# Output projection of a gated layer: weights stationary, 512 tokens of gated values moving, result written feature by token

## The chip, the core and the metric

The kernel runs on one core of one Trainium2 chip. The core has TensorE (PE) for matrix products into PSUM, with its weight loads shown apart (PEld), VectorE (DVE), ScalarE (ACT), GpSimd (POOL) and SyncE (SP), and 16 DMA engines that move data between HBM and SBUF. DMA transfers are issued here by SP and POOL. The metric is the device time of one execution in microseconds (us), median of several runs. The profile is of one further execution.

## The reference

Attention in chunks of 64 tokens, then two feed-forward layers on 4608 tokens of 512 features:

```python
attn = softmax(scale * q_c @ k_c.T); x = attn @ v_c        # chunks of 64
h = x @ w_in;  g = where(h > 0, h, exp(min(h, 0)) - 1)     # 512 -> 2048
x = g @ w_out                                              # 2048 -> 512
gate = 1 / (1 + exp(-(x @ w_gate)));  val = x @ w_val      # 512 -> 1536 each
out = (gate * val) @ w_out2                                # 1536 -> 512
```

The result is a float32 array of 4608 tokens by 512 features.

## The kernel before

Every product of the layers is computed with seven block products instead of eight (a Strassen scheme): both operands are cut in two halves each way, sums of the blocks are formed, and the seven results are added into four output blocks. The factors are float32, each split into a high part of type float32r and the rest; a product makes three passes (high x high, low weight x high, high weight x low), `PASSES` (line 34).

The weights are converted from float64 early on, summed for the seven products (`sums`, `sums_of_sums`, lines 249 to 272), split and written to DRAM (`wd`). `hold` (line 326) reads them back through POOL's queue ahead of their use, in tiles of 512 KB, up to `room` of them; all other tiles of at most 1024 float32 a partition (`four`) come out of the same 28 buffers (`w_p`), so `room(...)` is 28 less what those take. Larger tiles come out of ten slots of 2048 float32 (`get` and `free`, lines 362 to 370), which are handed round in turn; a tile in a slot waits until everything that used the slot before is done, a store from it too.

Tokens are worked in five blocks, four of 2 x 512 tokens and a last one of 2 x 256 (`NLS`, line 48).

- Stage 1, attention and the first layer, and stage 2, the second layer (`stage_2`, line 693). Its `product` (line 724) has the weights as the stationary operand and 512 tokens moving (256 in the short block). `split_b` makes the high part with a cast on ACT and the low part with a subtraction on DVE (`split`, line 99; the lines 95 and 101 in the profile), one product ahead of its use; `sub_b` makes the sums of blocks on DVE, `after` takes a finished product out of PSUM, and `beside` says what is issued after each part of a product. Everything is issued in the order in which the code calls it; each engine works in that order.
- Stage 3, the gated layer (`unit`, line 860): 30 units of seven products each; from unit 18 on units of 512 and of 256 tokens alternate. Unit 27 has 512 tokens, units 28 and 29 have 256. A unit ends with `finish` (line 944), which multiplies and stores the gated values to DRAM (`gvd`); it is run in the unit after, behind that unit's second product, on POOL for unit 28 and on DVE for 27 and 29. After each product `hold` is called with the room that the tiles of the moment leave.
- Stage 4, the output projection (`stages_3_4`, line 954). The block is cut into nine groups of 256 tokens (twice, for the two halves). Here the *gated values* are the stationary operand, 128 tokens at a time, and the weights move, 256 columns at a time (line 1022): 6 x 3 x 2 = 36 matmuls a product. A product fills one of the two banks of its PSUM tile, and groups take turns. `prepare` (line 983) makes the next product's split and sums just before a product is issued; a split is two tiles, one of 1024 and one of 512 elements a partition. The result is token by feature and is stored in rows of 2 KB. The first group's loads, sums and first split are placed into the last units of stage 3 (line 1064).

PSUM holds four tiles (`bank_x`, `w`, `y`, `z`) of two banks each; the seven products use x, w, y, z, x, y, z. A bank can be written again only when what it held has been read.

Of the kernel before, what the change touches and what calls it, by code (L numbers as in the profile page):

```python
# [18 lines left out]
DM = H * D  # L19
# [37 lines left out]
RIGHT = (0, 4, 3, 5, 1, 2, 6)  # L57
# [3 lines left out]
def kernel(  # L61
# [18 lines left out]
        for m, n in (("mid", QM), ("glu", QU), ("out2", QU // 2))  # L80
# [115 lines left out]
    def convert_pairs(which, queue_of):  # L196
# [52 lines left out]
        def sums(p):  # L249
            now[p, "s"] = alloc("s", F32)  # L250
            t, s = quarters(p, "t"), quarters(p, "s")
            if tiles_of[p][3]:
                nc.vector.tensor_add(out=s[:, 0], in0=t[:, 3], in1=t[:, 2])
                nc.vector.tensor_sub(out=s[:, 2], in0=t[:, 0], in1=t[:, 3])
            elif p < HF:
                nc.vector.tensor_add(out=s[:, 0], in0=t[:, 0], in1=t[:, 3])
                nc.vector.tensor_sub(out=s[:, 2], in0=t[:, 1], in1=t[:, 0])
            else:
                nc.vector.tensor_sub(out=s[:, 0], in0=t[:, 0], in1=t[:, 1])
                nc.vector.tensor_sub(out=s[:, 2], in0=t[:, 3], in1=t[:, 0])  # L260

        def sums_of_sums(p):
# [4 lines left out]
            elif p < HF:  # L267
                nc.vector.tensor_sub(out=s[:, 1], in0=s[:, 0], in1=t[:, 1])
                nc.vector.tensor_sub(out=s[:, 3], in0=t[:, 2], in1=s[:, 1])
            else:  # L270
                nc.vector.tensor_sub(out=s[:, 1], in0=t[:, 3], in1=s[:, 0])
# [51 lines left out]
    uses += 2 * [("out2", r, i) for i in range(7) for r in range(QU // 2)]  # L323
    held = {}

    def hold(at, room, ahead):
# [8 lines left out]
        for k in need:  # L335
            if not made(k):
                break
            if k not in held:
# [4 lines left out]
                nc.gpsimd.dma_start(out=t, in_=wd[m][q][:, (RIGHT if m == "out2" else LEFT)[i]])  # L343
# [349 lines left out]
    def stage_2(one):  # L693

        raw, gc, three = {}, {}, {}
        KEYS = {"b11": (0, 0), "b21": (1, 0), "b12": (0, 1), "b22": (1, 1)}
        FROM = ("b11", "t2", "b11", "b12", "b21", "b22", "b21")

        def load_b(j, k):
            if j is None:  # L700
                return
            par, h = KEYS[k]
            blk, c = divmod(START[j] + h * NLS[j], TB)
            for s in range(2):
                t = raw[j, k, s] = get(k, (HF // 2, NLS[j]))
                nc.sync.dma_start(out=t, in_=gd[blk][:, par, 4 * s:4 * s + 4, c:c + NLS[j]])

        def sub_b(j, out, a, b, s):
            if j is None:
                return  # L710
            if (j, out, s) not in raw:
                raw[j, out, s] = get(out, (HF // 2, NLS[j]))
            nc.vector.tensor_sub(out=raw[j, out, s], in0=raw[j, a, s], in1=raw[j, b, s])

        def split_b(j, i, p):
            if j is None:
                return
            for k in range(2):
                t = gc[j, i, 2 * p + k] = four(2, NLS[j], dtype=F32R)
                split(raw[j, FROM[i], p // 2][:, 2 * (p % 2) + k], t[:, 0], t[:, 1], nc.scalar, nc.vector)  # L720
            if i in (2, 3, 5, 6) and p % 2 == 1:
                free(raw.pop((j, FROM[i], p // 2)))

        def product(j, i, p):
            w = held["mid", p, i]
            for k in range(2):
                t = gc.pop((j, i, 2 * p + k))
                for u in range(2):
                    for n, (zw, zx) in enumerate(PASSES):
# [3 lines left out]
                            rhs=t[:, zx],  # L733
                            start=(i < 4 and p == 0 and k == 0 and n == 0),
                            stop=(p == QM - 1 and k == 1 and n == 2),
                            skip_group_check=True,
                        )

        def after(j, i):
            ps = bank[PRODUCTS[i]][:, :, 0:NLS[j]]  # L740

            def new(k):
                three[k] = shaped(three_p.tile([128, 1024], F32, tag="three", name=k), (2, NLS[j]))
                return three[k]

            def store(k, h, e):
                nc.sync.dma_start(out=ymid[j][:, h, e], in_=three.pop(k))
# [20 lines left out]
        def beside(j, nxt, i, p):  # L768

            h, odd = p // 2, p % 2 == 1  # L770
            if i == 0:
                if not odd:
                    sub_b(j, "t2", "b22", "b11", h)
                split_b(j, 1, p)
                if j == 0 and p == 3:
                    load_b(0, "b21")
            elif i == 1:
                split_b(j, 2, p)
                if odd:
                    sub_b(j, "b12", "b22", "b12", h)  # L780
            elif i == 2:
                if p == 0:
                    load_b(nxt, "b11")
                split_b(j, 3, p)
            elif i == 3:
                if p == 0:
                    load_b(nxt, "b12")
                split_b(j, 4, p)
            elif i == 4:
                if not odd:  # L790
                    sub_b(j, "b21", "b21", "t2", h)
                    free(raw.pop((j, "t2", h)))
                split_b(j, 5, p)
                if p == 3:
                    load_b(nxt, "b22")
            elif i == 5:
                if p == 0:
                    load_b(nxt, "b21")
                split_b(j, 6, p)
            else:  # L800
                split_b(nxt, 0, p)
                if odd:
                    sub_b(nxt, "b11", "b12", "b11", h)
# [18 lines left out]
        for n in range(HF):  # L822
            one(end - HF + n, True)
            if n in (0, 2, 4):
                load_b(0, ("b11", "b12", "b22")[n // 2])
            if 2 <= n <= 5:
                split_b(0, 0, n - 2)
            if n >= 6:
                sub_b(0, "b11", "b12", "b11", n - 6)
            hold(0, room(F1 - 2 * n - 2, 8), SLACK + 1 + n)  # L830
        for o, j in enumerate(ORDER):
            nxt = ORDER[o + 1] if o + 1 < NJ else None
            for i in range(7):
                for p in range(QM):
                    product(j, i, p)
                    if o == i == p == 0:
# [3 lines left out]
                        three_p = ctx.enter_context(  # L840
                            tc.tile_pool(name="three", bufs=3, side="right", reuse_waits="tile")
                        )
                    beside(j, nxt, i, p)
# [10 lines left out]
                after(j, i)  # L854
        assert not todo and not raw and not gc
# [296 lines left out]
```

## Time and profile before

| | us |
|---|---|
| median of three runs | 1652.19 (1652.01 to 1654.71) |
| profiled execution, in all | 1653.24 |
| its span in the trace | 1651.5 |
| TensorE busy | 1620.2 |
| VectorE busy | 1204.8 |
| ScalarE busy | 749.6 |
| GpSimd busy | 299.1 |

The span runs from the first to the last instruction that the trace shows; the profiled execution took 1.74 us more than that. The page of the profile lists busy time by engine, the span in 40 slices, the DMA queues, the chain of waits that ended last, and the costliest groups of instructions. The trace behind it can be asked for single stretches, lines, engines and transfers. Matmuls are pipelined, so that one matmul's duration is longer than the distance from its start to the next one's start.

### The profile page before, as it was taken

Reading aid. Unit: us, or ns where it says so; the run is one execution under the profiler, and the core shown is the slowest. Engines: PE = TensorE matmul, PEld = TensorE weight load, DVE = VectorE, ACT = ScalarE, POOL = GpSimd, SP = SyncE. Lnnn points to the kernel's source line nnn. Section 1 sums busy time; section 2 is a strip of 40 time slices with the busy share of each in tenths; the row PEclk is TensorE's granted clock in tenths of the full one; section 3 lists DMA queues with packets and bytes.
Section 4 is the critical chain, followed back from the end, with each engine's and each line's share of the span. In section 5 each row is a group of like instructions: output and inputs, shape, how many; then the busy total and the mean of one; then the engine's idle time right before and its main releaser. Section 6 shows DMA issues by size and latency. Waiting matters only on the chain.

```text
span 1651.5 us, 27371 instructions
## 1 busy us (share of the span) xinstructions
PE 1620.2 (98%) x10644; PEld 1385.6 (84%) x10644; DVE 1204.8 (73%) x1699; ACT 749.6 (45%) x1273; POOL 299.1 (18%) x488
## 2 busy tenths in 40 slices
PE   6899999999999999999999999999999999999998
PEld 4677777777788898888888888888888899999998
DVE  6878888888637689988855676776664457677676
ACT  5766767767644454463532242332321113333332
POOL 3332111122101022222121222222301030000000
PEclk9899999999999999999999999999999999999999
DMA  6568888898887689999699769779746497443531
GB/s 227 198 214 289 295 297 286 276 291 296 280 297 247 215 317 392 378 338 393 215 313 321 250 202 399 259 270 335 242 144 232 149 357 249 155 139 122 167 121 52
DMA packets 176417, 421.76 MB, mean 255 GB/s; under 512 B 13984, under 2 KB 54944, under 8 KB 171168
## 3 DMA queue, kind: packets, MB, share of 16 engines
q0 software_dynamic: 71328, 216.56, 39.4%
q1 hardware_dynamic: 104960, 203.45, 35.8%
q8 instruction: 84, 1.38, 0.3%
q14 instruction: 45, 0.37, 0.1%
HBM read 287.31 MB, written 132.64 MB: 254 GB/s over the span
## 4 chain that ended last, share of the span: by engine, by line
PE 74%; DVE 14%; ACT 8%; issue 2%; DMA 1%; POOL 0%; SPq 0%; ACTq 0%; DVEq 0%; POOLq 0%
PE bank_x L871 9%; PE bank_z L871 9%; PE bank_y L871 9%; PE bank_x L730 6%; PE bank_z L730 6%; PE bank_y L730 6%; PE bank_z L1022 5%; PE bank_x L1022 4%; PE bank_w L871 4%; PE bank_w L730 3%; PE bank_y L1022 3%; PE bank_y L401 3%; DVE elu L424 2%; PE bank_w L1022 2%; PE bank_z L401 2%
## 5 line engine op out<-in xcount | busy, mean ns | idle before, releaser
L95 ACT CAST four<-b 128x512 fp32r<-128x512 f32 (+1 forms) x240 | 128.0, 577 | 79.1 <-PE bank_y L730 20.8
L101 DVE TENSOR_TENSOR four<-b,four 128x512 fp32r<-128x512 f32 (+1 forms) x240 | 140.1, 634 | 30.2 <-ACT four L95 30.1
L871 PE MATMUL bank_z<-four,w 128*128 128x512 f32 (+1 forms) x720 | 157.6, 368 | 0.0
L893 ACT ACTIVATE s<-s 128x512 f32<-128x512 f32 (+1 forms) x60 | 35.4, 590 | 251.3 <-DVE s L104 251.3
L871 PEld LDWEIGHTS bank_z<-four,w 128*128 128x128 f32 x720 | 126.3, 189 | 22.5
L401 PE MATMUL bank_y<-xs,w 128*128 128x512 f32 x576 | 140.5, 399 | 1.4 <-POOL w L167 0.9
L401 PE MATMUL bank_w<-xs,w 128*128 128x512 f32 x576 | 140.7, 399 | 0.0
L401 PE MATMUL bank_z<-xs,w 128*128 128x512 f32 x576 | 139.6, 398 | 0.0
L343 POOL DMA_DIRECT2D w<-wd_glu x156 | 84.6, 546 | 300.7 <-PE bank_x L871 140.5
L401 PEld LDWEIGHTS bank_y<-xs,w 128*128 128x128 f32 x576 | 107.8, 191 | 23.7 <-POOL w L167 1.2
L401 PEld LDWEIGHTS bank_z<-xs,w 128*128 128x128 f32 x576 | 108.0, 191 | 22.0
L401 PEld LDWEIGHTS bank_w<-xs,w 128*128 128x128 f32 x576 | 107.4, 190 | 21.9
L343 POOL DMA_DIRECT2D w<-wd_mid x105 | 56.0, 537 | 265.9 <-PE bank_x L730 93.7
L730 PE MATMUL bank_x<-four,w 128*128 128x512 f32 (+1 forms) x480 | 100.2, 368 | 0.0
L730 PE MATMUL bank_y<-four,w 128*128 128x512 f32 (+1 forms) x480 | 100.2, 368 | 0.0
L730 PE MATMUL bank_z<-four,w 128*128 128x512 f32 (+1 forms) x480 | 100.2, 368 | 0.0
L730 PEld LDWEIGHTS bank_x<-four,w 128*128 128x128 f32 x480 | 83.7, 189 | 15.0
L730 PEld LDWEIGHTS bank_y<-four,w 128*128 128x128 f32 x480 | 83.7, 189 | 15.0
L730 PEld LDWEIGHTS bank_z<-four,w 128*128 128x128 f32 x480 | 83.7, 189 | 15.0
L104 DVE TENSOR_TENSOR s<-bank_z,s 128x1024 f32<-128x1024 f32 (+1 forms) x60 | 67.0, 1116 | 37.0 <-PE bank_z L871 35.7
L871 PE MATMUL bank_y<-four,w 128*128 128x512 f32 (+1 forms) x432 | 88.5, 354 | 0.0
L871 PE MATMUL bank_x<-four,w 128*128 128x512 f32 (+1 forms) x432 | 88.4, 354 | 0.0
(167 smaller groups left out, 3249.6 us busy)
## 6 DMA issues: line engine op xcount, KB each, us to landing
w<-wd_glu POOLq DMA_DIRECT2D x156, 512.0 KB, 8.2
w<-wd_mid POOLq DMA_DIRECT2D x105, 512.0 KB, 8.3
gd<-elu SPq DMA_DIRECT2D x72, 512.0 KB, 3.6
b<-gd SPq DMA_DIRECT2D x32, 1024.0 KB, 9.2
c<-gv SPq DMA_DIRECT2D x36, 768.0 KB, 5.4
wd_glu<-ch POOLq DMA_DIRECT2D x36, 512.0 KB, 4.8
raw<-in_qkv SPq DMA_DIRECT2D x61, 256.0 KB, 4.0
wd_mid<-ch POOLq DMA_DIRECT2D x24, 512.0 KB, 5.0
```

The costliest lines, as they stand in the source:

```text
L95: nc.scalar.copy(out=out, in_=raw)
L101: lo_eng.tensor_sub(out=lo, in0=raw, in1=hi)
L104: nc.vector.tensor_tensor(out=out, in0=a, in1=b, op=ALU.add)
L343: nc.gpsimd.dma_start(out=t, in_=wd[m][q][:, (RIGHT if m == "out2" else LEFT)[i]])
L401: nc.tensor.matmul(out=h_bank(d)[:, n], lhsT=w[:, zw, kk * 128:(kk + 1) * 128], rhs=xs[j, kk][:, zx], start=(kk == 0 and p == 0), stop=(kk ...
L424: nc.vector.scalar_tensor_tensor(out=e, in0=h_bank(d), scalar=0.0, in1=e, op0=ALU.max, op1=ALU.subtract,)
L730: nc.tensor.matmul(out=bank[PRODUCTS[i]][:, u, 0:NLS[j]], lhsT=w[:, k, zw, 128 * u:128 * u + 128], rhs=t[:, zx], start=(i < 4 and p == 0 a ...
L871: nc.tensor.matmul(out=ps[:, b], lhsT=w[:, b, zw, 128 * k:128 * k + 128], rhs=x_part(j, i, zx, k), start=(i < 4 and k == 0 and p == 0), st ...
L893: nc.scalar.activation(out=x, in_=x if of is None else of, func=ACTF.Sigmoid)
L1022: nc.tensor.matmul(out=po[c][:, m], lhsT=t[:, zx, q % 4, 128 * m:128 * m + 128], rhs=w[:, q % 2, zw], start=(i < 4 and q == 0 and p == 0 a ...
```

## The change

The second layer's routine becomes a class, `Seven`, with the layer's name, its number of weight tiles, and functions that say where a block is read and where a result is written. Stage 2 uses it with four parts, as before; stage 4 now uses it too, with three. In stage 4 the weights are thereby the stationary operand and 512 tokens of gated values move, and the result is feature by token: the kernel's output has the shape 512 by 4608 and is turned on the host when it is returned. The sums of `w_out2` follow the second layer's form (the third branch of `sums` and `sums_of_sums` goes), as many operations as before. A split in stage 4 is one tile of 2 x 512 in a slot, which is freed when its product has been issued. A block of gated values is loaded as a piece of four rows of tiles in a slot and a piece of two in a buffer of `w_p`. Three of those pieces are taken before the units end, so the room for weights in the last units shrinks by one to three. In the last units now stand three splits and a subtraction in two pieces.

```diff
+QO = F2 // 4
-        for m, n in (("mid", QM), ("glu", QU), ("out2", QU // 2))
+        for m, n in (("mid", QM), ("glu", QU), ("out2", QO))
...
-                nc.gpsimd.dma_start(out=t, in_=wd[m][q][:, (RIGHT if m == "out2" else LEFT)[i]])
+                nc.gpsimd.dma_start(out=t, in_=wd[m][q][:, LEFT[i]])
...
+    class Seven:
...
+        def tile(self, j, k, s):
+            n = 2 * min(2, self.parts - 2 * s)
+            return get(k, (n, NLS[j])) if n == 4 else four(n, NLS[j])
...
+        def split(self, j, i, p):
...
+            x = self.raw[j, FROM[i], p // 2][:, 2 * (p % 2):2 * (p % 2) + 2]
+            if self.parts == QM:
+                t = [four(2, NLS[j], dtype=F32R) for k in range(2)]
+                for k in range(2):
+                    split(x[:, k], t[k][:, 0], t[k][:, 1], nc.scalar, nc.vector)
+                self.gc[j, i, p] = t, None
+            else:
+                t = get("gc", (2, 2, NLS[j]), F32R)
+                split(x, t[:, :, 0], t[:, :, 1], nc.scalar, nc.vector)
+                self.gc[j, i, p] = [t[:, 0], t[:, 1]], t
...
+        def product(self, j, i, p):
+            w = held[self.m, p, i]
+            t, slot = self.gc.pop((j, i, p))
             for k in range(2):
                 for u in range(2):
                     for n, (zw, zx) in enumerate(PASSES):
                         nc.tensor.matmul(
                             out=bank[PRODUCTS[i]][:, u, 0:NLS[j]],
                             lhsT=w[:, k, zw, 128 * u:128 * u + 128],
-                            rhs=t[:, zx],
+                            rhs=t[k][:, zx],
...
+            if slot is not None:
+                free(slot)
...
-                parts = 8 + min(7, max(0, 7 * (n - JOINT) + i - 2))
+                parts = 8 + min(8, max(0, 7 * (n - JOINT) + i - 2))
                 if n >= END_WIDE:
-                    parts = 15 - 2 * max(0, i + 1 - XC) if n == END_WIDE else 8 if n == END_WIDE + 1 else 8 - i
+                    parts = (18 - 2 * max(0, i + 1 - XC), 11, 11 - i)[n - END_WIDE]
                 hold(MID + 7 * n + i + 1, room(parts), NW)
...
+        C = {"b21": 0, "b22": 1, "b12": 2, "b11": 3}
+
+        def keep(j, h, e):
+            c = START[j] + h * NLS[j]
+            return out[256 * e:256 * e + 256, c:c + NLS[j]].rearrange("(u p) n -> p u n", p=128)
+
+        z = Seven("out2", QO, lambda j, k, q: gvd[j][:, C[k], q], keep)
         N = len(seq)
         beside = {
-            (N - 4, 0): lambda: load_g(0, "c12"),
-            (N - 3, 0): lambda: load_g(0, "c22"),
-            (N - 3, 4): lambda: load_g(0, "c11"),
-            (N - 2, 0): lambda: load_g(0, "c21"),
-            (N - 2, 3): lambda: sum_1(0),
-            (N - 1, 1): lambda: sum_2(0),
-            (N - 1, 4): lambda: split_g(0, 0, "c11", keep=True),
+            (N - 4, 0): lambda: z.load(0, "b11"),
+            (N - 3, 0): lambda: z.load(0, "b12"),
+            (N - 3, 4): lambda: z.load(0, "b22"),
+            (N - 2, 3): lambda: z.split(0, 0, 0),
+            (N - 2, 5): lambda: z.split(0, 0, 1),
+            (N - 1, 1): lambda: z.split(0, 0, 2),
+            (N - 1, 3): lambda: z.sub(0, "b11", "b12", "b11", 0),
+            (N - 1, 5): lambda: z.sub(0, "b11", "b12", "b11", 1),
         }
...
-        for g in range(G):
+        for j in range(NJ):
+            nxt = j + 1 if j + 1 < NJ else None
             for i in range(7):
-                prepare(g, i)
-                product(g, i)
-                after(g, i)
-                if g == 0:
-                    hold(MID + 7 * N + 3 * (i + 1), room(7), NW)
-                while pending:
-                    pending.pop(0)()
+                for p in range(QO):
+                    z.product(j, i, p)
+                    while pending:
+                        pending.pop(0)()
+                    z.beside(j, nxt, i, p, j == 0)
+                    if j == 0:
+                        hold(MID + 7 * N + 3 * i + p + 1, room(7), NW)
+                z.after(j, i)
...
-    args.append(nc.dram_tensor("out_0", (NT, DM), F32, kind="ExternalOutput").ap())
+    args.append(nc.dram_tensor("out_0", (DM, NT), F32, kind="ExternalOutput").ap())
...
-    return r.results[0]["out_0"]
+    return np.ascontiguousarray(np.asarray(r.results[0]["out_0"]).T)
```

`load`, `sub`, `beside` and `after` of the class are the old functions of stage 2 with the number of parts as a variable.

## Rows read from the trace of the kernel before

**Rows 1.** The page's busy time, share and instructions of each engine.

```profile
PE 1620.2 (98%) x10644; PEld 1385.6 (84%) x10644; DVE 1204.8 (73%) x1699; ACT 749.6 (45%) x1273; POOL 299.1 (18%) x488
```

**Rows 2.** Windows of stages 2 and 4: stretch, length, each engine's busy us.

```profile
core 0: us, PE busy (x) PEld busy (x) DVE busy (x) ACT busy (x) POOL busy (x), PEclk, DMA share, GB/s
505.60:852.00 346.40, 346.40 (x1688) 293.76 (x1687) 292.57 (x394) 172.84 (x319) 70.53 (x130) 1.00 0.90 312
...
1371.00:1647.20 276.20, 275.13 (x2268) 272.70 (x2268) 199.77 (x209) 105.39 (x145) 0.00 (x0) 1.00 0.41 136
```

**Rows 3.** Chain of waits, stages 3 and 4: start, us, what, matmuls.

```profile
1273.72 2.72 PE bank_w L871 x12
...
1351.19 1.44 PE bank_y L871 x12
...
1380.96 4.32 PE bank_y L1022 x36
```

**Rows 4.** The same chain at the passage from stage 3 to 4.

```profile
1362.54 4.41 DMA gv<-s
...
1369.87 1.05 ACT gc L95
```

**Rows 5.** DMA issues at 1353.2, 1353.8 and 1362.5: count, KB, us to landing.

```profile
gv<-s SPq DMA_DIRECT2D x1, 512.0 KB, 8.6
gv<-t SPq DMA_DIRECT2D x1, 512.0 KB, 11.8
...
gv<-s SPq DMA_DIRECT2D x1, 256.0 KB, 7.3
```

**Rows 6.** Groups by line and shape in stage 4: busy, mean ns, idle before.

```profile
L1022 PEld LDWEIGHTS bank_z<-w,gc 128*128 128x128 f32 x432 | 53.6, 191 | 2.2 <-DVE gc L101 2.2
...
L101 DVE TENSOR_TENSOR gc<-c,gc 128x1024 fp32r<-128x1024 f32 x36 | 44.0, 1221 | 36.1 <-ACT gc L95 36.1
L95 ACT CAST gc<-c 128x1024 fp32r<-128x1024 f32 x35 | 36.7, 1049 | 42.6 <-DVE c L992 42.6
...
L101 DVE TENSOR_TENSOR four<-c,four 128x512 fp32r<-128x512 f32 x36 | 24.7, 686 | 0.0
```

**Rows 7.** Groups by line and shape in stage 2.

```profile
L713 DVE TENSOR_TENSOR b<-b,b 128x2048 f32<-128x2048 f32 x15 | 34.3, 2288 | 0.2
...
L104 DVE TENSOR_TENSOR c<-bank_y,u 128x1024 f32<-128x1024 f32 x8 | 9.8, 1220 | 1.1 <-PE bank_y L730 1.1
...
L713 DVE TENSOR_TENSOR b<-b,b 128x1024 f32<-128x1024 f32 x4 | 4.9, 1222 | 0.1
```

**Rows 8.** Timeline of the last two units: start, us, engine, line, operation.

```profile
1354.43 0.69 DVE L104 TENSOR_TENSOR s<-bank_z,s 128x512 f32<-128x512 f32 x1
1355.04 1.75 DVE L977 TENSOR_TENSOR s<-c,c 128x1536 f32<-128x1536 f32 x1
...
1361.97 2.85 DVE L981 TENSOR_TENSOR s<-s,c 128x1536 f32<-128x1536 f32 x1
...
1366.26 0.42 ACT L893 ACTIVATE s<-s 128x256 f32<-128x256 f32 x1 [5.76 <-DVE s L104]
...
1366.98 0.42 DVE L907 TENSOR_TENSOR t<-bank_x,t 128x256 f32<-128x256 f32 x1 [0.76 <-ACT t L893]
1367.02 1.60 PE L871 MATMUL bank_z<-four,w 128*128 128x256 f32 x12
...
1370.82 0.61 ACT L95 CAST four<-c 128x512 fp32r<-128x512 f32 x1
...
1370.96 0.73 PE L1022 MATMUL bank_x<-w,gc 128*128 128x256 f32 x4 [2.35 <-ACT gc L95]
```

**Rows 9.** The end: timeline of the last eviction, and the stores' issues by line.

```profile
1647.15 0.69 DVE L104 TENSOR_TENSOR four<-bank_z,four 128x512 f32<-128x512 f32 x1 [3.62 <-PE bank_z L1022]
...
L1043 SPq DMA_DIRECT2D out<-four x36: 332/351/1256, 1400.0 to 1648.3; - x36
```

**Rows 10.** Windows in the last units, with the DMA share ahead of GB/s.

```profile
1348.00:1358.00 10.00, 10.00 (x85) 9.96 (x84) 7.54 (x9) 2.13 (x5) 4.17 (x8) 1.00 1.13 409
1363.00:1368.00 5.00, 5.00 (x43) 4.90 (x42) 3.54 (x4) 0.69 (x2) 1.92 (x5) 1.00 1.12 402
```

More of the change, by code (lines that the diff above doesn't have):

```diff
@@ L56 @@
 LEFT = (0, 4, 3, 5, 1, 6, 2)
-RIGHT = (0, 4, 3, 5, 1, 2, 6)
 @with_exitstack
@@ L691, in done_x, with __init__, pieces, load @@
             free(xt.pop((j, n)))
[L693 to L699, printed above, removed]
+    KEYS = {"b11": (0, 0), "b21": (1, 0), "b12": (0, 1), "b22": (1, 1)}
+    FROM = ("b11", "t2", "b11", "b12", "b21", "b22", "b21")
+    class Seven:
+        def __init__(self, m, parts, fetch, keep):
+            self.m, self.parts, self.fetch, self.keep = m, parts, fetch, keep
+            self.raw, self.gc, self.three = {}, {}, {}
+        def tile(self, j, k, s):
+            n = 2 * min(2, self.parts - 2 * s)
+            return get(k, (n, NLS[j])) if n == 4 else four(n, NLS[j])
+        def pieces(self):
+            return range((self.parts + 1) // 2)
+        def load(self, j, k):
@@ L700, in load_b @@
             if j is None:
                 return
[L702 to L708, printed above, removed]
+            for s in self.pieces():
+                t = self.raw[j, k, s] = self.tile(j, k, s)
+                nc.sync.dma_start(out=t, in_=self.fetch(j, k, slice(4 * s, 4 * s + t.shape[1])))
@@ L716, in split_b, with ends @@
+        def ends(self, p):
+            return p % 2 == 1 or p == self.parts - 1
+        def split(self, j, i, p):
             if j is None:
                 return
-            for k in range(2):
[L719 to L727, printed above, removed]
+            x = self.raw[j, FROM[i], p // 2][:, 2 * (p % 2):2 * (p % 2) + 2]
[4 more added lines that the diff above has]
+                self.gc[j, i, p] = t, None
+            else:
+                t = get("gc", (2, 2, NLS[j]), F32R)
+                split(x, t[:, :, 0], t[:, :, 1], nc.scalar, nc.vector)
+                self.gc[j, i, p] = [t[:, 0], t[:, 1]], t
+            if i in (2, 3, 5, 6) and self.ends(p):
+                self.release(j, FROM[i], p // 2)
@@ L766, in after, with beside @@
                 store("u", 0, 1)
-        def beside(j, nxt, i, p):
-            h, odd = p // 2, p % 2 == 1
+        def beside(self, j, nxt, i, p, first):
+            h, starts, ends, last = p // 2, p % 2 == 0, self.ends(p), p == self.parts - 1
             if i == 0:
[L772 to L776, printed above, removed]
+                if starts:
+                    self.sub(j, "t2", "b22", "b11", h)
+                self.split(j, 1, p)
+                if first and last:
+                    self.load(j, "b21")
@@ L788, in beside @@
-                split_b(j, 4, p)
+                    self.load(nxt, "b12")
+                self.split(j, 4, p)
             elif i == 4:
[L790 to L795, printed above, removed]
+                if starts:
+                    self.sub(j, "b21", "b21", "t2", h)
+                    self.release(j, "t2", h)
@@ L796, in beside @@
+                self.split(j, 5, p)
+                if last:
+                    self.load(nxt, "b22")
             elif i == 5:
                 if p == 0:
[L798 to L803 removed]
+                    self.load(nxt, "b21")
+                self.split(j, 6, p)
+            else:
+                self.split(nxt, 0, p)
+                if ends:
+                    self.sub(nxt, "b11", "b12", "b11", h)
@@ L853, in stage_2 @@
                     hold((7 * o + i) * QM + p + 1, room(8, 8 if todo or last else 0), 10)
-                after(j, i)
-        assert not todo and not raw and not gc
+                z.after(j, i)
+        assert not todo and not z.raw and not z.gc
     pending = []
```

162 lines of the change are left out of this document (35 added, 127 removed).

## The prediction

> **What bounds the kernel now.** I read the page's busy times first, then the busy time by stage, then the chain of waits, and only then the groups and the timeline around the output projection. The page says that TensorE is busy 98% of the span [rows 1]. The windows by stage say it again for the stage in question: in the output projection PE is busy 275.1 of 276.2 us at a granted clock of 1.00 (the 2.4 GHz level), DVE 199.8, ACT 105.4, and the DMA share is 0.41. The second layer, whose routine is to be used, has PE busy for all of its 346.4 us [rows 2]. So the time is PE's, and a busy PE is not a PE at its peak: the question is how long one matmul stands in the way of the next. The chain shows this directly, because its PE pieces follow each other without a gap. Twelve 512-column matmuls take 2.72 us (0.2267 us each), twelve 256-column ones of the gated layer 1.44 us (0.120 each), and 36 of the output projection, all of 256 columns, 4.32 us (0.120 each) [rows 3]. Two lengths give a line: 0.1067 us for 256 columns, 0.4167 ns each, and 13.3 ns that every matmul costs whatever its length.
>
> Two smaller losses stand beside that. Once per group PE waits for the low half of a split that DVE finishes late; the nine groups lose 2.2 us so, as the row of the weight loads has it [rows 6]. And between the gated layer and the projection PE stands: its last gated piece starts at 1367.02 and ends 1.44 later at about 1368.4, the first product starts at 1370.96 [rows 8]. The chain says why: the first split's cast on ACT began at 1369.87 [rows 4]. Its slot was that of s of the last unit but one (unit 28 of 0 to 29), whose store was issued at 1362.54 and took 7.3 us to land [rows 5]: 1369.84. From 1368.4 to PE's end at 1647.15 [rows 9] are 278.7 us, of which 2268 x 0.120 = 272.2 are matmuls at their pitch and 0.2 the end of the last one; 6.4 are waits; beside the 2.6 and 2.2 just named the rest is small waits for late low halves in the first group.
>
> **The columns.** Before: 9 groups x 7 products x 36 = 2268 matmuls of 256 columns. After: a product has 3 parts x 2 k x 2 u x 3 passes = 36 matmuls, 4 blocks of 7 x 36 with 512 columns (1008) and one block with 256 (252). The columns are the same, 580,608; 1008 matmuls fewer are issued. 1008 x 0.2267 + 252 x 0.120 = 228.5 + 30.2 = 258.7 us, so **13.4 us less**, which is 1008 x 13.3 ns.
>
> What follows is said by the Trainium skill, not by a row. The page "TensorE: Matmul & The Clock Gate" (section "Back-to-back issue gap") gives a warm gap of N/2.4 + 2.5 ns. That speaks against this change: by it the 1008 matmuls saved would be worth 2.5 us and not 13.4. The rows here disagree with it (120.0 and 226.7 ns where it gives 109.2 and 215.8), so I go by the rows and keep what it gives as a rival's price.
>
> **The steady state.** Does the new routine keep PE fed? Per product of a wide block PE works 36 x 0.2267 = 8.16 us. DVE's work in a wide block: 21 low halves at 1.22 [rows 6], four subtractions in two pieces at 2.29 + 1.22, and five evictions at 1.22 [rows 7], together 25.6 + 14.0 + 6.1 = 45.8 of 57.1 us; ACT has 21 casts at 1.05 [rows 6], 22 us, and two copies. Each split stands a whole product ahead of its use. The worst product is the first: eviction 1.22 after the previous product's end, subtraction 2.29, cast 1.05, low half 1.22 make 5.8 us before the first part of the next product is ready, with 8.16 to do it in; the third part is ready at 10.7 and needed at 8.16 + 5.44 = 13.6. In the narrow block: 0.69 + 1.22 + 0.6 + 0.69 [rows 6 to 8], some 3.9 us with the eviction's lag, against 4.32. So it fits, narrowly at the end. The slots: ten, of which five hold raw blocks and three splits, so a split takes a slot that was freed two or three parts before, not the one being read. PSUM: a bank is now filled by one product without a second half to alternate with, but it is written again two products later at the earliest. In place of the nine waits of 2.2 us I put 0.3: nearest is the second layer, the same routine with four parts for three, where PE never waits [rows 2]. The bounds are 0 and the old 2.2. The loads change from 1 KB rows to 8 KB runs and have the same bytes; the DMA share of 0.41 [rows 2] covers them. The store of 512 tokens by feature has 2 KB rows as before.
>
> **The junction.** The change moves three splits and two subtractions in front of PE's first product: splits into unit 28 after products 3 and 5 and into unit 29 after product 1, subtractions after products 3 and 5 of unit 29. Out go a sum of 1.75 and one that took 2.85 while POOL worked beside it [rows 8], and the first split. Behind what do they queue? ACT and DVE work in order. In unit 28 the second low half stands ahead of the last eviction: from the eviction that begins at 1354.43 [rows 8] on, sigmoid, first cast, low half, multiply and the next eviction end at about 1359.0; then sigmoid 0.42, second cast 1.05, low half 1.22, eviction 0.69: 1362.4. ACT's copy that opens unit 29 comes behind that unit's last sigmoid: 1363.4; cast 1364.45, low half 1365.7, eviction of y 1366.4. PE wants bank y again at 1365.4 and waits **1.0**. Eviction of z 1367.1, subtraction 1369.4, the multiply that frees bank x 1369.8; PE's first product wants it at 1369.4 and waits **0.5**. After that: the last unit's finish, the subtraction t2, cast and low half end at 1378.5, and the second product asks at 1378.0 and, for the low half, 0.45 later: **0.1**. So 1.6 us where there are 2.6 now. The unknown is the third split's slot. By the order of gets and frees in the code it is one of unit 27's two, whose stores landed at 1353.2 + 8.6 = 1361.8 and 1353.8 + 11.8 = 1365.6 [rows 5], in a stretch where the DMA engines are full [rows 10]; I take the first, which costs nothing. With the second the cast waits to 1365.6 and the same steps give 3.5 us; with unit 28's s (1369.84), 7.8. Below, an undisturbed junction gives 0. The weights: 1 to 3 fewer are held through the last units and two are fetched twice; the second fetch is over 20 us ahead of its use, against landings of 7 to 12 us [rows 5], so nothing. In the first block a weight is needed every 2.72 us and not 1.44.
>
> **The end.** From PE's end 4.35 us pass: an eviction of 0.69, two stores of 256 KB whose issues take 0.35 each, the landing [rows 9]. After, the same eviction and one store: one issue less, 0.35, so 4.0.
>
> **The sum**, in the profiled execution's time: 1368.4 + 1.6 + 258.7 + 0.3 + 0.2 = 1629.2 for PE's end, + 4.0 = 1633.2 of span, 18.3 less than 1651.5. That execution took 1653.24 in all, 1.74 more than its span, and lies 1.05 above the median of the three runs, 1652.19. So 1652.2 - 18.3, rounded: **1634.0 us**.
>
> **The rivals.**
> - *The store's landing takes the place of the late split.* The third split gets a slot whose store lands late; ACT is stopped, behind it DVE's evictions, and PE waits for a bank. For it: that is how the junction is lost now [rows 4, 5], with DMA full [rows 10]; and b12 is twice the load that c22 was. Against it: the finish of unit 27 comes a unit earlier than the store that hurts now. 3.5 to 7.8 us in place of 1.6: 1636 to 1640.
> - *The fixed cost is not the matmul's.* The 13.3 ns might lie in something that the longer matmul keeps, such as its operands' reads: then 1008 fewer matmuls give nothing and only waits (6.4 - 1.6 - 0.3 = 4.5) and the end (0.35) are left: 1647. Against it: the pitch of 0.2267 stands in the gated layer at the same operand types [rows 3]. By the Trainium skill's section named above it would be 1645.
> - *Slower: DVE becomes the bound.* If slots run short, a cast can't run ahead, and DVE waits out each cast: 45.8 + 21 x 1.05 = 67.9 us in a wide block instead of 57.1, with the narrow one 48 us in all: 1682. It decides the sign when a block passes 57.1 + 18.2/4 = 61.6 us, that is when 15 of 21 casts are uncovered. Against it: two slots to spare, and no wait of PE in the second layer [rows 2].
> - *The change doesn't do what it says*: shorter or more matmuls than counted, 1652. The loop bounds speak against it.
>
> **How the numbers follow.** Forecast, 1631 to 1636.5: 0.62. Late landing, 1636.5 to 1640: 0.22. Something between, from several small waits, 1640 to 1648: 0.08. The fixed cost, 1647: 0.03. No change: 0.02. DVE the bound: 0.03. About 0.2% (3.3 us) is what a measurement of this kernel can tell from no change. Faster 0.95, same 0.02, slower 0.03. The range 1631 to 1640 reaches from the sum without any wait at the junction and in the blocks (1632, and 1 us for the spread of runs) to the latest landing.
>
> **What would show it.** Right: 1008 matmuls of 512 columns at 0.2267 in the chain, a product of 8.16 us, no PE wait inside a block, PE idle under 2 us between 1360 and 1372, one store last. Wrong: a PE piece at another pitch, a split's cast that waits for a store, a low half that PE waits for in each block.

## The result and the profile after

The changed kernel takes 1636.45 us in the median of five executions (1633.37 to 1638.73), the kernel before 1652.20 beside it: a ratio of 0.9900, 95% interval 0.9886 to 0.9914. Two further sets of executions of the same changed kernel gave 1635.04 and 1636.11 (below). One execution of the second set took 6276 us, for a reason that nothing here shows, and 1635.04 is the median of its other three. The forecast was 1634.0, the range 1631 to 1640. The profiled execution of the changed kernel is the longest of the five, 1638.73 in all with a span of 1636.9.

The page's busy times (engine, us, share of the span, instructions), to be laid beside [rows 1]:

```profile
PE 1602.9 (98%) x9636; PEld 1330.7 (81%) x9636; DVE 1200.1 (73%) x1662; ACT 749.1 (46%) x1244; POOL 303.8 (19%) x491
```

TensorE issues 9636 matmuls and not 10644: the 1008 that the prediction counted are gone, and PE is busy for 17.3 us less. The chain of waits (start, us, what, matmuls), from unit 28 to the end, shows both the gain and a new loss; [rows 3] and [rows 4] are its counterpart:

```profile
1346.04 1.43 PE bank_x L902 x12
...
1364.66 0.49 POOL s L977
...
1367.49 1.72 POOL t L979
1369.23 8.84 DMA gv<-t
...
1378.18 1.05 ACT gc L95
1379.23 0.04 issue
1379.27 1.22 PE bank_w L747 x2
1380.49 0.04 issue
1380.53 9.98 PE bank_w L747 x34
1390.51 8.16 PE bank_y L747 x36
...
1602.67 4.31 PE bank_x L747 x36
...
1632.94 0.69 DVE u L104
```

From 1390.51 on this is what was forecast: 26 wide products of exactly 8.16 us each and seven narrow ones of 4.31 to 4.33, without a gap, then one eviction and one store. 26 x 8.16 + 7 x 4.32 = 242.4, and 1390.51 + 242.4 = 1632.91. The span ends 4.0 after that.

Ahead of it stands the loss. Unit 28's first product starts at 1346.04. Its seven products and the seven of unit 29 take 14 x 1.44, the first two products of the projection 2 x 8.16, together 36.5 us; so the third product could start at 1382.5 and starts at 1390.51. These 8.0 us are the measure used below, "the loss at the passage": from the start of unit 28 to the third product of the projection, less 36.48. The timeline (start, us, engine, line, operation; in brackets the idle time before and what ended it) shows how they arise:

```profile
1362.72 0.53 POOL L337 DMA_DIRECT2D w<-wd_out  x1 [1.53 <-DMA w<-wd_out]
...
1364.11 2.28 DVE L720 TENSOR_TENSOR b<-b,b 128x2048 f32<-128x2048 f32 x1
1364.11 0.53 POOL L337 DMA_DIRECT2D w<-wd_out  x1 [0.86 <-DMA w<-wd_out]
...
1364.66 2.87 POOL L977 TENSOR_TENSOR s<-s 128x512 f32<-128x512 f32 x1
...
1367.49 1.71 POOL L979 TENSOR_TENSOR t<-t 128x256 f32<-128x256 f32 x1
...
1374.98 2.29 DVE L720 TENSOR_TENSOR t<-b,b 128x2048 f32<-128x2048 f32 x1 [4.26 <-issue]
...
1378.18 1.99 ACT L95 CAST gc<-t 128x1024 fp32r<-128x1024 f32 x2 [8.51 <-DMA gv<-t]
...
1379.27 2.05 PE L747 MATMUL bank_w<-gc,w 128*128 128x512 f32 x3 [4.04 <-ACT gc L95]
```

POOL stands in front of a weight's fetch (L337) until an earlier one has landed, and the finish of unit 28 (L977, L979) is queued behind. The earlier one is the eighth before it: the fetches of 1358.72, 1360.66 and 1362.72 begin 0.51 us after the eighth before each has landed (1358.21, 1360.15, 1362.21), that of 1364.11 0.28 after (1363.83). None of the 429 transfers that POOL issues in this profile begins before the eighth ahead of it has landed, so POOL never has more than eight under way. The finish begins at 1364.66, and its two multiplications take 2.87 and 1.71 us beside DVE's subtraction. So the stores of unit 28's s and t are issued at 1367.56 and 1369.23. The DMA issues (count, KB, us to landing) give what they took:

```profile
gv<-s SPq DMA_DIRECT2D x1, 256.0 KB, 7.3
...
gv<-t SPq DMA_DIRECT2D x1, 256.0 KB, 8.8
```

The slots that s and t leave go to the projection's second subtraction (t2) and to the first split of its second product. The first store lands at 1367.56 + 7.3 = 1374.9, and the subtraction starts at 1374.98; the second at 1369.23 + 8.8 = 1378.0, and the cast starts at 1378.18. TensorE wanted that split at 1374.94 and could start only at 1379.27, 4.3 us later (4.0 of them idle by the row); then its weight loads wait 0.8 for the low half. What comes on top is in the windows (length, each engine's busy us with instructions, then the granted clock, the DMA share and GB/s):

```profile
1370.00:1375.00 5.00, 5.00 (x24) 3.99 (x22) 0.74 (x3) 0.00 (x0) 2.94 (x6) 1.00 1.12 394
1375.00:1380.00 5.00, 0.96 (x4) 0.50 (x2) 3.02 (x2) 1.82 (x2) 0.53 (x1) 0.79 1.11 388
1380.00:1385.00 5.00, 4.96 (x13) 3.55 (x12) 3.84 (x4) 2.34 (x4) 0.00 (x0) 0.52 1.09 398
...
1391.00:1632.90 241.90, 241.90 (x1186) 205.29 (x1184) 178.90 (x156) 95.15 (x105) 0.00 (x0) 1.00 0.36 128
```

After the wait of 4.0 us the granted clock fell: 0.52 in the next 5 us is nearly all at the lower level, 1.2 GHz. The 34 matmuls took 9.98 us. At their pitch they are 34 x 0.2267 = 7.71; in the second set's profile (below) the same 34, behind the same wait for a low half but with the clock at 1.00, took 8.04. So 0.3 us go with the restart and 1.9 with the lower clock. With the waits for banks y and x ahead of the first product, 0.3 and 0.4, the 8.0 us are accounted for: 0.7 + 4.3 + 0.8 + 0.3 + 1.9. In the last window, 241.9 us long, PE is busy throughout at a clock of 1.00.

### The profile page after: what moved, and what is told of

It reads as the page before. It is cut to its first block, busy times and chain, and to the rows that moved or that the text cites. A ratio compares the mean times of both kernels' runs of the same rounds, so it can differ in the third digit from the quotient of the medians.

```text
span 1636.9 us, 25299 instructions
## 1 busy us (share of the span) xinstructions
PE 1602.9 (98%) x9636; PEld 1330.7 (81%) x9636; DVE 1200.1 (73%) x1662; ACT 749.1 (46%) x1244; POOL 303.8 (19%) x491
## 4 chain that ended last, share of the span: by engine, by line
PE 75%; DVE 12%; ACT 8%; issue 2%; DMA 2%; POOL 0%; SPq 0%; ACTq 0%; DVEq 0%; POOLq 0%
PE bank_z L747 11%; PE bank_y L747 11%; PE bank_x L747 10%; PE bank_x L902 9%; PE bank_y L902 9%; PE bank_z L902 9%; PE bank_w L747 5%; PE bank_w L902 5%; DVE elu L418 2%; PE bank_z L395 2%; PE bank_y L395 2%; PE bank_w L395 2%; DVE s L488 1%; ACT elu L413 1%; DVE m L487 1%
## 5 line engine op out<-in xcount | busy, mean ns | idle before, releaser
L337 POOL DMA_DIRECT2D w<-wd_glu x159 | 86.1, 545 | 301.7 <-PE bank_x L902 115.1
L337 POOL DMA_DIRECT2D w<-wd_mid x105 | 56.0, 537 | 265.8 <-PE bank_x L747 83.1
```

Of the source, the lines that this page charges most:

```text
L337: nc.gpsimd.dma_start(out=t, in_=wd[m][q][:, LEFT[i]])
```

## The experiments

**The columns.** Is it really the number of matmuls that pays? Here the output projection issues each 512-column matmul as two of 256; all else is as in the changed kernel.

```diff
+                        step = 256 if self.m == "out2" else NLS[j]
+                        for o in range(0, NLS[j], step):
...
-                            out=bank[PRODUCTS[i]][:, u, 0:NLS[j]],
+                                out=bank[PRODUCTS[i]][:, u, o:o + step],
...
-                            rhs=t[k][:, zx],
+                                rhs=t[k][:, zx, o:o + step],
```

> The changed kernel with every 512-column matmul of the output projection issued as two of 256 columns, weights still stationary: 1008 matmuls more for the same columns. If 13.3 ns are the price of each matmul whatever its columns, a product takes 8.64 us instead of 8.16 and the time grows by 13.4 us: 1650. If the gain of the change came from which operand is stationary, or from waits alone, the pitch of a pair stays 0.2267 us and the time 1636.5.

Measured: 1648.82 us (11 executions), ratio to before 0.9976 (0.9967 to 0.9986), so 12.4 above the changed kernel's median. The chain:

```profile
1369.70 8.64 PE bank_x L749 x72
...
1602.98 8.64 PE bank_z L749 x72
1611.62 4.32 PE bank_x L749 x36
```

Each of the 28 wide products takes 8.64 and not 8.16 us: 72 x 0.120. 28 x 0.48 = 13.4 us, the term of the prediction to the tenth. What is left of the gain with halves, 0.24% or 4.0 us (2.3 to 5.5), is everything but the columns. The forecast had 18.3 - 13.4 = 4.9 for that. The rival in which the longer matmul keeps the fixed cost has fallen. Not separated is the matmul's own cost from that of its weight load: each half has a load of its own (2010 for 2011 matmuls from 1391 to 1632, with PEld busy throughout), so the 13.3 ns are those of a matmul together with its load.

In this kernel's profile another thing happened at the passage, seen again below in smaller measure: POOL's finish met the third split's low half on DVE.

```profile
1361.28 3.15 DVE L101 TENSOR_TENSOR gc<-four,gc 128x1024 fp32r<-128x1024 f32 x1 [0.26 <-ACT gc L95]
1361.36 1.30 POOL L979 TENSOR_TENSOR s<-s 128x512 f32<-128x512 f32 x1
...
1365.08 2.93 PE L904 MATMUL bank_y<-four,w 128*128 128x256 f32 x12 [2.04 <-DVE s L104]
```

The low half took 3.15 us (1.23 in the changed kernel's profile at the same place), the evictions behind it were late, and PE waited 2.0 us for bank y.

**The late stores.** If the loss at the passage is the late finish of unit 28, three ways of having it earlier should each take it away. The first has it done by DVE:

```diff
-            eng = nc.gpsimd if n % QU == QU - 2 else nc.vector
+            eng = nc.gpsimd if n % QU == QU - 2 and n != len(seq) - 2 else nc.vector
```

> The changed kernel with one edit: the finish of unit 28 (two multiplications and two stores) on VectorE instead of GpSimd. Theory A: PE's wait ahead of the second output product comes from unit 28's two stores, issued at 1367.6 and 1369.2 and landing 7.3 and 8.8 us later, because the subtraction t2 and the first split sit in the slots that they leave. Then the stores go out at about 1362.5, the second product starts within 1 us of the first one's end, PE's clock doesn't fall, and some 7 us are won, less about 1.1 us because VectorE's two multiplications delay the last evictions: 1630.5. Theory B: the steps themselves (finish of unit 29, subtraction, cast, low half) are too long for one product of 8.16 us. Then the wait stays at about 4 us and the time is 1637.

Measured: 1634.15 us, ratio 0.9888 (0.9875 to 0.9902). The second leaves it on POOL and lets at most nine of the projection's weights be held ahead, so that fewer fetches stand before it:

```diff
-    def hold(at, room, ahead):
+    def hold(at, room, ahead, out2=NW):
...
+        need = [k for k in need if k[0] != "out2"] + [k for k in need if k[0] == "out2"][:out2]
...
-                hold(MID + 7 * n + i + 1, room(parts), NW)
+                hold(MID + 7 * n + i + 1, room(parts), NW, 9)
...
-                        hold(MID + 7 * N + 3 * i + p + 1, room(7), NW)
+                        hold(MID + 7 * N + 3 * i + p + 1, room(7), NW, 9)
```

> The changed kernel with at most 9 of the 21 output weights fetched ahead, from unit 19 to the end of the first block. Theory A': the stores land late because the 21 weight tiles that are fetched ahead fill the DMA engines, and they are issued late because GpSimd's finish stands behind weight issues that wait. Then the two stores land in 3 to 5 us instead of 7.3 and 8.8, the finish starts by about 1361 instead of 1364.7, no wait is left ahead of the second product, and the time is 1629 to 1631. If the landing has nothing to do with the weights, the time stays at 1636.5. If 9 tiles are too few, PE waits for a weight in the first block and the time is above 1637.

Measured: 1632.45 us, ratio 0.9881 (0.9867 to 0.9896). The stores did leave earlier, but did not land faster: 8.0 and 11.5 us, with the DMA engines as full as before (402 GB/s from 1360 to 1370, 394 in the ten us after). The limit only changed the order: the finish waited for no fetch, and POOL issued four fetches right behind it, from 1364.89. The third issues the finish before the fetches of unit 29's first product:

```diff
+            if n == len(seq) - 1 and i == 0:
+                while pending:
+                    pending.pop(0)()
```

> The changed kernel with the finish of unit 28 issued behind the first product of unit 29 and ahead of that step's weight fetch, not behind the second product's; it stays on GpSimd. Theory A: the multiplications then start at about 1361 instead of 1364.7, the stores are issued some 4 to 5 us earlier and land by about 1371 and 1373; the wait ahead of the second product shrinks from 4.3 us to under 1 and the clock holds: 1629.5 to 1631. Theory B: 1636.5.

Measured: 1633.34 us, ratio 0.9888 (0.9874 to 0.9902). All three medians lie 1.5 to 3.7 us above what was expected: the expectations started from the loss of 8.0 us in the first profile, and two further profiles of the changed kernel show a smaller one. No execution of the changed kernel was on the same chip as these three, and some of their executions overlap with its. The second set of the changed kernel was measured later, on one chip with the versions called paced and moved below:

> The changed kernel as it is, for a second profile and for times on the same chip as the runs beside it. If the wait ahead of the second product hangs on when GpSimd gets past its weight issues, it differs between executions: PE waits there for anything from 0 to 5 us, and the median lies between 1634 and 1637.

Measured: 1635.04 us (1634.59 to 1636.13), ratio 0.9893 (0.9878 to 0.9908). Its profile has the same wait as the first one, but smaller:

```profile
1363.45 1.42 POOL L977 TENSOR_TENSOR s<-s 128x512 f32<-128x512 f32 x1
...
1365.60 0.36 SPq L980 DMA_DIRECT2D gv<-t  x1
...
1376.44 2.00 ACT L95 CAST gc<-t 128x1024 fp32r<-128x1024 f32 x2 [5.60 <-DMA gv<-t]
1377.54 0.30 PEld L747 LDWEIGHTS bank_w<-gc,w 128*128 128x128 f32 x2 [1.39 <-ACT gc L95]
...
1378.80 8.04 PE L747 MATMUL bank_w<-gc,w 128*128 128x512 f32 x34 [0.53 <-DVE gc L101]
```

The store of t left at 1365.60 and landed 10.7 us later, at 1376.3; the cast follows, and the weight loads of the second product wait 1.4 us for it. So the loss is not one number: it is 8.0 us in the first profile and 3.4 in this one. Of the difference the cast makes 2.7, by when POOL gets past its fetches and how long its multiplications take beside DVE's work, and the clock 1.9.

**The same finish in the kernel before.** There the first split also waits for a store of unit 28. Had the kernel before gained as much from the finish on DVE, the late stores would not belong to the change.

```diff
-            eng = nc.gpsimd if n % QU == QU - 2 else nc.vector
+            eng = nc.gpsimd if n % QU == QU - 2 and n != len(seq) - 2 else nc.vector
```

> The kernel before, with the finish of unit 28 on VectorE instead of GpSimd. If the 2.6 us that PE stands between the gated layer and the projection in the kernel before come from the landing of that unit's store, which the first split's slot waits for, the store goes out 1 us or so earlier at most (GpSimd begins it at 1361.2 there, hardly late), and lands correspondingly little earlier: 0 to 1.5 us won, 1651 to 1652.3. A gain of 2 us or more would say that GpSimd's slowness, not the landing, set that wait.

Measured: 1653.60 us in 11 executions beside 1653.05, ratio 1.0007 (0.9998 to 1.0016): nothing. In the kernel before POOL started the finish at 1361.20, 12.9 after the start of unit 28 at 1348.32, right behind two fetches that had waited 0.9 us for a product. So POOL was not behind there, although it was fetching. On DVE the store left 14.4 us after the start of unit 28; on POOL it was 14.2, at 1362.54 [rows 4]. There was nothing to gain.

**The traffic.** Would the stores land sooner if the weights for the first block were not fetched as fast as buffers allow? Beside the limit of nine, each fetch of the first block is held back by a copy of one column out of the split just made, on POOL.

```diff
...
-                        hold(MID + 7 * N + 3 * i + p + 1, room(7), NW)
+                        t, _ = z.gc[(0, i + 1, p) if i < 6 else (1, 0, p)]
+                        nc.gpsimd.tensor_copy(out=pad[:, 0:1], in_=t[0][:, 0, 0:1].bitcast(F32))
+                        hold(MID + 7 * N + 3 * i + p + 1, room(7), NW, 9)
```

> The changed kernel with at most 9 output weights fetched ahead, and in the first block each further fetch held back on GpSimd by a copy of one column of the split just made, so that fetches go at the pace of the products (about one in 2.7 us). Theory A': unit 28's stores land 8 to 12 us after their issue because fetches that nobody needs yet fill the DMA engines. Then they land in 3 to 6 us, the DMA share between 1370 and 1380 falls below 0.8, the first split's cast waits for the subtraction and no longer for a store, and the loss at the junction (against 14 x 1.44 + 2 x 8.16 us) is 1 to 2 us: 1632. If the landing hangs on something else, it stays at 8 to 12 us.

Measured: 1633.20 us, ratio 0.9880 (0.9866 to 0.9893). Two windows of this kernel, columns as above:

```profile
1360.00:1370.00 10.00, 9.20 (x69) 8.54 (x68) 8.68 (x10) 2.95 (x6) 2.00 (x2) 1.00 0.98 353
1370.00:1380.00 10.00, 10.00 (x46) 8.28 (x45) 7.42 (x8) 3.28 (x4) 2.84 (x4) 1.00 0.57 199
```

These executions took 1631.98 to 1633.93, those of the changed kernel on this chip 1634.59 to 1636.13. The DMA share from 1370 to 1380 falls from 1.11 in the changed kernel's profile to 0.57, and both stores land after 7.3 us. The 3 to 6 us of the expectation were too few: the fetches issued earlier were still being served up to 1370. But the cast now follows the subtraction, not the store, and TensorE does not wait for the second product:

```profile
1374.49 2.00 ACT L95 CAST gc<-t 128x1024 fp32r<-128x1024 f32 x2 [3.34 <-DVE t L721]
```

**The rest of the passage.** With the finish early, the other small waits are bank y's and bank x's. The third split is moved behind unit 29's third product, out of POOL's way, and the first piece of the subtraction behind the fifth:

```diff
...
-            (N - 1, 1): lambda: z.split(0, 0, 2),
-            (N - 1, 3): lambda: z.sub(0, "b11", "b12", "b11", 0),
+            (N - 1, 2): lambda: z.split(0, 0, 2),
+            (N - 1, 4): lambda: z.sub(0, "b11", "b12", "b11", 0),
```

> The changed kernel with unit 28's finish issued behind the first product of unit 29, the third split behind its third product instead of the second and the first subtraction piece behind the fifth instead of the fourth. With the early finish alone PE lost 1.5 us at the junction: 0.8 for bank y behind the third low half, 0.4 for bank x behind the subtraction. Both waits should be gone, the loss under 0.7 us, 1632.3 in the median. If the steps moved back make the second product late, its wait shows instead and nothing is won.

Measured: 1632.74 us (1632.37 to 1633.08, again clear of the changed kernel on the same chip), ratio 0.9878 (0.9864 to 0.9891). No wait is left ahead of the projection's first product. The second still loses 1.3 us, where under 0.7 in all was expected: the subtraction behind the last unit's finish makes its cast and its low half late. Then the last unit's finish is also put behind the subtraction t2, alone and together with the held-back fetches:

```diff
...
+                    z.beside(j, nxt, i, p, j == 0)
                     while pending:
                         pending.pop(0)()
-                    z.beside(j, nxt, i, p, j == 0)
```

> As b1_moved, and in the output projection the finish of the last unit is issued behind the second product's first preparation (subtraction t2 and first split) instead of ahead of it. In b1_moved the first product started without a wait and the second lost 1.2 us to the chain last eviction, sigmoid, the two multiplications of the finish, subtraction, cast, low half. Without the multiplications in it (and the wait for their sigmoid) the subtraction starts 1.4 us earlier. If the store of unit 28's t then lands in time (it took 10.9 us in b1_moved, to about 1374), the loss at the junction is under 0.5 us and the time 1631.5 to 1632; if the store is the later one, the cast still waits for it and nothing is won over 1632.7.

> As b4_last_late, and the weight fetches of the first block paced as in e5_paced, where the stores landed 7.3 us after their issue. Then no store is late, the second product waits for nothing, and the junction's loss is under 0.3 us: 1631 to 1631.8.

Measured: 1633.40 us, ratio 0.9883 (0.9868 to 0.9897), and 1633.43, ratio 0.9886 (0.9868 to 0.9904). Both are 1.4 to 1.6 us above what was expected. In the first one's profile the cast still follows the store of t, and the loss is 1.3 us as before, so nothing was won by it. In the second one's TensorE waits for nothing at the passage. The medians of these versions don't rank by what their passages still lose, 0 to 2 us: they lie between 1632.4 and 1634.2, and executions of one kernel are 0.7 to 4.3 us apart. Part of that comes from stages that no version changes: the start of unit 28 lies between 1345.8 and 1348.8 in the profiles of the changed kernel and its versions.

**Is the loss given back later?** The last comparison sets the changed kernel beside the version without waits, on one chip.

> The changed kernel once more, beside the version with paced fetches and both finishes moved, on the same chip. Theory (the passage from stage 3 to 4 loses 3 to 8 us of TensorE's time, by how late GpSimd issues unit 28's stores): 1635 to 1637 us, 2 to 4 above the other. Rival (the loss at the passage is given back later, so that the median doesn't hold it): the two within 1 us of each other.

> The version without any wait of TensorE at the passage, once more, beside the changed kernel on the same chip. Theory: 1632 to 1634 us, 2 to 4 below the changed kernel. Rival (the loss is given back later): within 1 us of it.

Measured: 1636.11 us (1635.22 to 1638.16; ratio 0.9901, 0.9885 to 0.9918) and 1631.33 (1630.31 to 1633.42; ratio 0.9870, 0.9856 to 0.9885). The executions of the two don't overlap; the medians are 4.8 us apart, somewhat more than expected. The size is not settled by this: the same version had 1633.43 in its first set, on another chip, which is 1.6 to 3.0 below the changed kernel's three medians. The chain of the version has one TensorE piece behind the other through the passage:

```profile
1367.01 1.44 PE bank_z L903 x12
1368.45 8.19 PE bank_x L748 x36
1376.64 8.29 PE bank_w L748 x36
1384.92 8.16 PE bank_y L748 x36
```

Eleven profiles side by side (the kernel with halves has longer products and is left out). Times in us after the start of unit 28's first product:

| kernel | finish begins | store of t issued | second product's cast | loss at the passage |
|---|---|---|---|---|
| changed, first profile | 18.6 | 23.2 | 32.1 | 8.0 |
| changed, third set | 16.2 | 18.6 | 29.5 | 5.0 |
| changed, second set | 16.5 | 18.6 | 29.5 | 3.4 |
| finish on DVE | 15.2 | 16.4 | 28.1 | 2.1 |
| nine ahead | 14.2 | 16.2 | 27.8 | 1.7 |
| finish early | 14.2 | 16.2 | 27.6 | 1.5 |
| moved | 14.2 | 16.2 | 27.4 | 1.3 |
| paced | 14.2 | 16.2 | 27.3 | 1.4 |
| moved, last finish late | 14.2 | 16.2 | 27.2 | 1.3 |
| paced, both finishes moved, last set | 14.2 | 16.2 | 26.1 | 0.2 |
| paced, both finishes moved, first set | 14.2 | 16.2 | 25.8 | 0.0 |

Undisturbed, the second product wants its cast to begin at 14 x 1.44 + 8.16 - 1.05 = 27.3. The loss falls as the cast comes down to that. What is left there, 1.3 to 1.5 us in four versions, are waits for banks y and x or for a low half. Two rows with the same cast, 29.5, differ by 1.6 us: that is the clock, for the 34 matmuls took 9.60 us in the one and 8.04 in the other. The windows of the two (the third set first) have it at 0.84 and at 1.00 from 1375 to 1380:

```profile
1375.00:1380.00 5.00, 3.45 (x11) 2.16 (x10) 3.50 (x3) 2.03 (x3) 0.00 (x0) 0.84 1.12 391
```

```profile
1375.00:1380.00 5.00, 3.50 (x14) 2.25 (x14) 2.49 (x4) 2.00 (x2) 0.53 (x1) 1.00 1.12 391
```

## Why the prediction held, and where it failed

**Columns: right.** 13.4 us were forecast. The chain has 8.16 and 4.32 us per product throughout, and the kernel with halves puts 13.4 of product time back. The Trainium skill's gap of N/2.4 + 2.5 ns ("TensorE: Matmul & The Clock Gate", section "Back-to-back issue gap"), by which the change would have been worth an estimated 2.5 us here, does not hold for these matmuls: 226.7 ns at 512 columns and 120.0 at 256 were measured after the change too. The Trainium skill gives that gap for an isolated matmul; for a stream with weight loads the same section has about 131 ns at 512 columns, which these rows don't show either.

**Steady state: right.** 0.3 us were put in, none was lost. PE is busy for all of the 241.9 us behind the third product. DVE has 178.9 us of work there, so it is not the bound, and the rival in which it is the bound has fallen.

**The end: right.** 4.0 us were forecast and 4.0 measured, against 4.35 before [rows 9].

**The junction: wrong.** 1.6 us were forecast; 8.0, 5.0 and 3.4 were measured in three profiles. Of the forecast's terms, bank y (1.0) and bank x (0.5) were there, at 0.3 and 0.4 us in the first profile. The one that failed is the last, "the subtraction t2, cast and low half end at 1378.5 ... 0.1". That sentence works out when the engines would be free. It does not ask which slots t2 and the second product's first split take. The question was asked of the third split alone, and there the answer taken (a store long landed) was right. The two tiles that come after it in the handing round take unit 28's s and t, and those stores were the late ones already in the kernel before [rows 4, 5]. A second step failed with it. The weights were set at nothing, since each fetch lies 20 us ahead of its use. That holds for the weights, though they landed after 7 to 16 us from unit 28 on and not after 7 to 12; but POOL waits in front of such a fetch while eight others are under way, and unit 28's finish is queued behind it. In the kernel before it began 12.9 us after the start of unit 28, in the changed kernel 16.2 to 18.6; with the fetches out of the way, 14.2, right behind a sigmoid on ACT. A third term was missing altogether, the clock: 1.9 us in the first profile, 1.6 in the third, none in the second.

**The rivals.** The late landing, 1636 to 1640, came in part: the mechanism, a split's cast that waits for a store, is the one that it named, in the wrong tile. The median, 1636.45, lies on the border between it and the forecast. The prediction's own sign of being wrong, a split's cast that waits for a store, came true, behind the stretch from 1360 to 1372 that it meant to watch. The forecast's mechanism carried the sign and most of the size, 15.8 of 18.2 us; that the median fell on the forecast's side of the border, by 0.05 us, is luck.

**The sum, on the first profile.** The forecast span was 1633.2. The loss at the passage adds 8.0 - 1.6 = 6.4. Unit 28 started at 1346.04 instead of 1348.32, which takes 2.3 off and lies within the spread of that start over the profiles (1345.8 to 1348.8 in the changed kernel and its versions, 1347.1 and 1348.3 in the two of the kernel before), and the unused 0.3 of the steady state goes too. 1633.2 + 6.4 - 2.3 - 0.3 = 1637.0; measured were 1636.9.

## What to carry to other kernels

When work is moved ahead of the point at which an engine would run dry, follow every tile that it takes, not the first one alone: list the slots in the order in which they are handed round, and for each one the store that must land before it is free. Here GpSimd, which issues the fetches, stood still while eight of them were under way, and whatever was queued behind, a finish and its store, was late by as much; count the transfers under way as well as the buffers. The gain of longer matmuls came out as two pitches in the chain had it; the price of the passage is where this forecast went wrong.

## What the runs showed of the hardware

- **GpSimd beside VectorE.** POOL's multiplication takes 1.30 us and took 2.87 when DVE's subtraction of 2.28 had begun 0.55 us before it. The other way round the low half on DVE, 1.23, took 3.15 though it had begun 0.08 before POOL's. The Trainium skill ("SBUF — State Buffer", section "SBUF: two separate sides") says that whichever of the two starts first keeps the port they share and the other blocks. The first case agrees: counted from the end of the subtraction, the multiplication took 1.14. In the second the one that started first, by these rows, was the one that lost; but 0.08 us is little, and the profile's times of POOL are rough, so this does not decide against the Trainium skill.
- **Eight fetches under way.** In the first profile of the changed kernel and in six others (the kernel before, the second and third set, finish on DVE, nine ahead, both finishes moved) no transfer that POOL issues begins before the eighth ahead of it has landed; the shortest distance is 0.28 us. Whether the chip or the program's queue sets the eight, these runs don't show.
- **The clock after a short wait.** After 4.0 us without a matmul the clock was granted at 0.79 and then 0.52. In two other profiles the same waits of 1.0 and 0.5 us in the second product had 0.84 and 0.82 granted in the one case and 1.00 in the other. Why they differ, these runs don't show.
- **Landing in a full queue.** At some 400 GB/s a store of 256 KB landed 7 to 12 us after its issue, with the fetches paced 5.9 to 8.6. Issuing it earlier made it land earlier, but by less: the store of t left at 18.6 and landed 10.7 us later, left at 16.2 and landed 10.9 to 11.5 us later.
